# Retention and MLP on one core: the scores of two chunks issued back to back, the second pair of PSUM banks taken from the MLP ring

## The chip, the cores and the metric

The kernel runs on one core of a Trainium2 chip. A core has TensorE (PE: matmuls into PSUM; weight loads are listed as PEld), VectorE (DVE), ScalarE (ACT), GpSimd (POOL) and SyncE (SP, which here only issues DMAs). PSUM has eight banks of 128 x 512 fp32 values. Each engine takes its instructions in order, and engines wait for one another on semaphores. The metric is the device time of one execution in microseconds (us).

## The reference, cut to what matters

There are 4 batches of 768 positions. The first half is a retention layer with 8 heads of 64 dimensions; the second a low-rank mix along the sequence and an MLP of 512 to 2048 to 512 with a residual.

```
state = gamma[h] * state + outer(k[:, :, t], v[:, :, t])      # for each t
y[:, :, t] = q[:, :, t] @ state / sqrt(64)
x = y with the heads side by side                             # (4, 768, 512)
u = x + (x.T @ U @ V).T
out = u + relu(u @ w_ch1) @ w_ch2
```

The kernel computes the retention in six chunks of 128 positions: with q and k scaled by powers of gamma, a chunk's output is its causally masked scores (k times q) applied to v, plus q applied to the state that the chunks before have summed up.

## The kernel before, in words

Batch 0 has its own start, in blocks of 256 positions. After it the program runs four rounds, b = 1 to 4 (the last `for` of the function). A round computes the MLP of batch b - 1 as a list of pieces (`mlp_pieces`), and the steps of the retention and the low-rank part of batch b are put between the pieces. `weave` does this by position: each piece has a cost in us as written in the code, each step a mark given as a share of the round, and a step is issued ahead of the first piece that begins at or after its mark. So the order of the instructions is fixed in the program, and nothing is rearranged at run time.

Five kinds of step belong to a chunk `(b, ci)`. `prep_chunk` scales and casts q, k and v on GpSimd (L267, L269) from tiles of the ring `in`, which the SP queue fills. `turn_dma` (L433) makes `qkT` from `qkd` by a transposing DMA; in batch 2 it is issued by ScalarE's queue, in batch 3 by SP's. `state` (L445) adds the chunk to the state in PSUM and copies it out on ScalarE (L85). `score` (L461) makes eight matmuls of 64 rows by 128, one for each head, even heads into one PSUM bank and odd heads into another; two operations on VectorE then multiply each bank by the causal mask and write `a0` and `a1` (L466). `mix` makes four matmuls of q with the state (L476) and eight of `a` with v (L481) in one bank, and ScalarE copies that to `x` (L85). All other matmuls in these stages use the full 128 rows, except those of the low-rank part (L499, L512).

The MLP's pieces: an up piece is four matmuls into one bank (L678), 512 positions wide or 256 wide, and a relu that writes `gT`: every fourth relu is on VectorE (L683), the others on ScalarE (L685); in round 1 it is every third. From batch 1 on the down product is made with seven block products in place of eight (L600), for which VectorE makes sums and differences of `gT` blocks (`g_sums`, L553, tiles `gS` and `gT`). These sums are chained to certain up pieces.

PSUM is dealt out by hand: `bank(tag)` rotates through a list of banks. In rounds 2 to 4 the ring `mlp` has the banks 6, 0, 1 and 2, `s` has 3 and 4, `o` has 5 and `st` has 7; the down products A, B and C use 6 and 0, 1, and 2. A matmul that starts a new use of a bank waits for the last reader of the use before.

The marks of round b are in `at` (one for each chunk) and `lag` (for the steps `state`, `score` and `mix` of a chunk). The change touches the score, the relu's choice of engine and the marks:

```
at = [0.04 + 0.085 * i for i in range(NCK)]
lag = [0.12, 0.17, 0.23] if b == 2 else [0.1, 0.12, 0.2]
```

Of the kernel before, what the change touches and what calls it, by code (L numbers as in the profile page):

```python
# [18 lines left out]
def kernel(  # L19
# [52 lines left out]
    def bank(tag, dtype=fp32):  # L72
        n_bank[0] += 1
        ring = RINGS[tag]
        ring.append(ring.pop(0))
        return psum.tile([P, 2048 // (4 if dtype == fp32 else 2)], dtype,
                         tag=f"bank{ring[-1]}", name=f"{tag}_{n_bank[0]}",
                         bufs=1)

    def four(t):  # L80
        return t.rearrange("p (n m) -> p n m", n=4)
# [147 lines left out]
    for i in range(NST):  # L229
        t = consts.tile([P, 4, P], bf16, name=f"state{i}")  # L230
# [3 lines left out]
    def causal(t):  # L234
        return t[:, None, :].to_broadcast([P, 4, P])
# [217 lines left out]
                evac("A", ns[r, :, r], four(st_p)[r, :, r])  # L453
            live["state", b] = ns

    def score(b, ci):
        vb, qkT, state = live[b, ci]
        sp = [bank("s") for _ in range(2)]
        for h in range(H):
            r = ds(D * (h % 2), D)  # L460
            nc.tensor.matmul(sp[h % 2][:, ts(h // 2, P)], qkT[r, 4 + h // 2],  # L461
                             qkT[r, h // 2], start=True, stop=True)
        for i in range(2):
            a = rmid.tile([P, 4, P], bf16, tag=f"a{i}", bufs=2,
                          name=f"a{i}_{b}_{ci}")
            nc.vector.tensor_tensor(a, four(sp[i]), causal(mask), op=ALU.mult)  # L466
            live[b, ci].append(a)

    def mix(b, ci):
        if ci == 0:  # L470
# [81 lines left out]
    def part(f, *args):  # L552
        return lambda: f(*args)  # L553
# [8 lines left out]
    def chain(*fs):  # L562
        def f():
            for g in fs:
                g()
        return f
# [100 lines left out]
    def mlp_pieces(b):  # L667
        gT = gtp.tile([P, NM, S], fp16, tag="gT", name=f"gT_{b}")
        pieces = []
        n = [0]  # L670

        def up(m, lo, sz):
            j, nj = lo // P, sz // P

            def f():
                g_p = bank("mlp")
                for c in range(NCB):
                    nc.tensor.matmul(g_p[:, :sz], w1b[:, c, ts(m, P)],  # L678
                                     uTs[b][:, ds(j, nj), c],
                                     start=(c == 0), stop=(c == NCB - 1))  # L680
                n[0] += 1
                if n[0] % (3, 4, 4, 4)[b] == 0:
                    nc.vector.tensor_relu(gT[:, m, ds(lo, sz)], g_p[:, :sz])  # L683
                else:
                    nc.scalar.activation(gT[:, m, ds(lo, sz)], g_p[:, :sz],  # L685
                                         AF.Relu)
            return f

        lo = [(0.864, up(m, 0, LO)) for m in range(NM)]
        hi = [(0.432, up(m, LO, S - LO)) for m in range(NM)]  # L690
        if b < SEVEN:
            pieces += lo + hi
        else:
            gS = gtp.tile([P, 3, NH, TH], fp16, tag="gS", name=f"gS_{b}")

            def quad(t, i):
                return [t[i], t[i + 1], t[i + NH], t[i + NH + 1]]

            def late(steps, at, fs):
                for i, f in enumerate(fs):  # L700
                    cost, g = steps[at + i]
                    steps[at + i] = (cost, chain(g, f))

            for t, i in ((lo, 0), (lo, 2), (hi, 0), (hi, 2), (lo, 4), (hi, 4),
                         (lo, 6), (hi, 6)):
                pieces += quad(t, i)
            late(pieces, 12, g_sums(gT, gS, 0))
            late(pieces, 16, g_sums(gT, gS, 2))
            late(pieces, 24, g_sums(gT, gS, 4))
            s1, s2, s3, s4 = g_sums(gT, gS, 6)  # L710
            late(pieces, len(pieces) - 1, [chain(s1, s2)])
            down = down_pairs(b, gT, gS)
            late(down, 0, [s3, s4])
            return pieces + down
        hold = {}

        def down(j, m0):
            def f():
                if m0 == 0:
                    hold[j] = bank("mlp")  # L720
                ch = hold[j]
                for m in range(m0, m0 + 4):
                    nc.tensor.matmul(ch, gT[:, m, ts(j, P)], w2b[:, m],  # L723
                                     start=(m == 0), stop=(m == NM - 1))
                if m0 == NM - 4:
                    o_sb = outp.tile([P, DM], fp32, tag="o_sb",
                                     name=f"o_{b}_{j}")
                    nc.vector.tensor_tensor(o_sb, ch, us[b][:, j], op=ALU.add)
                    dst = out[b, ts(j, P)]
                    if b:  # L730
                        stores.append((nc.scalar, dst, o_sb))
                    else:
                        for i in range(2):
                            stores.append((nc.sync, dst.rearrange(
                                "(p two) c -> two p c", two=2)[i],
                                o_sb[ds(HP * i, HP)]))
            return f

        for j in range(NCK):
            for m0 in range(0, NM, 4):  # L740
                pieces.append((0.864, down(j, m0)))
        return pieces
# [108 lines left out]
    for b in range(1, B + 1):  # L851
        tracks = []
        if b > 1:
            old = b - 1 < SEVEN
            first = [part(lr_expand, b - 1, 4, 2, "qk" if old else "st"),
                     part(lr_turn_pe, b - 1, 4, "qk" if old else "o")
                     if b < 3 else part(lr_turn, b - 1, 4)]
            if not old:
                RINGS["mlp"] = [6, 0, 1, 2]
        tracks.append((first, 0.02, (0.2, 0.14, 0.1, 0.06)[b - 1]))  # L860
        if b < B:
            if b == 1:
                at = [0.475, 0.575, 0.63, 0.69, 0.745, 0.8]
                lag = [0.01, 0.035, 0.065]
                turn = turn_pe
                for i in range(AHEAD, NCK):
                    tracks.append(([part(prep_chunk, b, i)], at[i] - 0.1, 1))
                tracks.append(([order_v], at[-1] - 0.05, 1))
                for f, d in zip(w2_sums(0) + w2_sums(2),
                                (0.515, 0.53, 0.55, 0.6, 0.655, 0.67, 0.715,  # L870
                                 0.73)):
                    tracks.append(([f], d, d))
            else:
                for i in range(NCK):
                    prep_chunk(b, i)
                at = [0.04 + 0.085 * i for i in range(NCK)]
                lag = [0.12, 0.17, 0.23] if b == 2 else [0.1, 0.12, 0.2]
                if b == 2:
                    for i, f in enumerate(w2_sums(4) + w2_sums(6)):
                        d = 0.04 + 0.025 * i  # L880
                        tracks.append(([f], d, d))
                turn = turn_dma
            for i in range(NCK):
                for f, d in ((turn, 0), (state, lag[0]), (score, lag[1]),
                             (mix, lag[2])):
                    tracks.append(([part(f, b, i)], at[i] + d, at[i] + d))
            t = at[-1] + lag[2]
            if b == 1:
                tracks += [([part(lr_open, b), part(lr_proj, b)], t + 0.02,
                            t + 0.02),  # L890
                           ([part(lr_expand, b, 0, 4)], t + 0.04, t + 0.04),
                           ([part(lr_turn_pair, b, 0, "A"),
                             part(lr_turn_pair, b, 2, "D")], t + 0.08, t + 0.12)]
            else:
                for fs, d in (([part(lr_open, b), part(lr_proj, b)], 0.03),
                              ([part(lr_grow, b, 0, 4, "st")], 0.06),
                              ([part(lr_add, b, 0, 4, (0, 1))], 0.06),
                              ([part(lr_add, b, 0, 4, (2, 3))], 0.11),
                              ([part(lr_turn, b, 0)], 0.17),
                              ([part(lr_turn, b, 2)], 0.171)):  # L900
                    tracks.append((fs, t + d, t + d))
        weave(mlp_pieces(b - 1), *tracks)
# [29 lines left out]
```

## Time and profile before

Four executions were timed; the profiled one took the same time as the lowest of them.

| what | value |
|---|---|
| median of 4 runs | 224.35 us |
| lowest and highest | 223.83 and 226.71 us |
| the profiled execution | 223.83 us |
| its span from first to last instruction | 221.2 us |
| round 2's up pieces (MLP of batch 1, chunks of batch 2) | about 82 to 109 us, chunks up to 118 us |
| round 3's up pieces (MLP of batch 2, chunks of batch 3) | about 131 to 157 us, chunks up to 165 us |
| eight score matmuls, L461, each | 216 ns, two at a time |
| mask, L466, 128 x 512 | 680 ns (median) |
| relu of 512 columns: ScalarE L685, VectorE L683 | 597 ns, 686 ns (mean, 82 to 170 us) |
| sums of 128 x 768, L553 | about 550 ns |

In the lines of a timeline the first number is the start in us from the start of the span, the second the length; then engine, line, operation, what is written and read, the shape, and how many instructions are merged. In brackets stands how long the engine was idle before, and what ended that. Matmuls overlap, and their ends are modelled, so starts tell more than lengths. ACTq and SPq are the queues of ScalarE and SP that issue DMAs. In a group of the page, "128*128" is the size of the array that a matmul uses and the next figures its operand.

### The profile page before, as it was taken

Reading aid. Unit: us, or ns where it says so; the run is one execution under the profiler, and the core shown is the slowest. Engines: PE = TensorE matmul, PEld = TensorE weight load, DVE = VectorE, ACT = ScalarE, POOL = GpSimd, SP = SyncE. Lnnn points to the kernel's source line nnn. Section 1 sums busy time; section 2 is a strip of 40 time slices with the busy share of each in tenths; the row PEclk is TensorE's granted clock in tenths of the full one; section 3 lists DMA queues with packets and bytes.
Section 4 is the critical chain, followed back from the end, with each engine's and each line's share of the span. In section 5 each row is a group of like instructions: output and inputs, shape, how many; then the busy total and the mean of one; then the engine's idle time right before and its main releaser. Section 6 shows DMA issues by size and latency. Waiting matters only on the chain. (4 is left out here: it accounts for less than half of the span.)

```text
span 221.2 us, 5593 instructions
## 1 busy us (share of the span) xinstructions
PE 214.0 (97%) x2275; PEld 151.3 (68%) x2275; DVE 142.7 (65%) x293; ACT 88.4 (40%) x182; POOL 85.4 (39%) x123
## 2 busy tenths in 40 slices
PE   7989999999999999999999999999999999999993
PEld 7868854485656554666788874766888846668882
DVE  7488665335766378699795843886868452857542
ACT  3247545465464315567611015666320035550000
POOL 6458888778779665325658202000000000000000
PEclk9999999999999999999999999999999999999999
DMA  6999999999999999999999499720002731000123
GB/s 168 302 279 282 286 373 261 365 334 204 214 220 222 197 233 213 277 189 197 240 206 213 161 229 234 143 50 0 3 0 98 190 123 22 0 1 3 47 105 133
DMA packets 93369, 38.82 MB, mean 176 GB/s; under 512 B 76864, under 2 KB 86176, under 8 KB 93344
## 3 DMA queue, kind: packets, MB, share of 16 engines
q1 hardware_dynamic: 86144, 35.33, 67.9%
q10 hardware_dynamic: 7200, 3.15, 7.1%
q8 instruction: 17, 0.28, 0.6%
q14 instruction: 8, 0.07, 0.1%
HBM read 27.46 MB, written 6.29 MB: 153 GB/s over the span
## 5 line engine op out<-in xcount | busy, mean ns | idle before, releaser
L678 PE MATMUL mlp<-uT,w1b 128*128 128x512 f16 (+1 forms) x512 | 89.6, 326 | 0.2 <-DMA uT<-x 0.2
L685 ACT ACTIVATE gT<-mlp 128x512 f16<-128x512 f32 (+1 forms) x94 | 45.6, 491 | 63.1 <-PE mlp L678 59.3
L678 PEld LDWEIGHTS <-w1b 128*128 128x128 f16 x512 | 48.0, 98 | 30.7 <-DMA uT<-x 0.7
L683 DVE TENSOR_SCALAR gT<-mlp 128x512 f16<-128x512 f32 (+1 forms) x34 | 18.9, 555 | 27.4 <-PE mlp L678 27.4
L600 PEld LDWEIGHTS <-gT 128*128 128x128 f16 x288 | 27.6, 98 | 3.6
L466 DVE TENSOR_TENSOR a<-s,mask 128x512 bf16<-128x512 f32 x36 | 23.1, 683 | 8.8 <-PE s L461 8.8
L269 POOL TENSOR_TENSOR qkd<-in,gk 128x512 bf16<-128x512 f32 x18 | 19.2, 1066 | 18.1 <-DMA in<-in_k_dram 17.6
L723 PE MATMUL mlp<-w2b,gT 128*128 128x512 f16 x96 | 24.1, 380 | 0.0
L269 POOL TENSOR_TENSOR qkd<-in,gq 128x512 bf16<-128x512 f32 x18 | 19.4, 1080 | 11.9 <-DMA in<-in_q_dram 10.1
L600 PEld LDWEIGHTS <-gS 128*128 128x128 f16 x216 | 20.9, 98 | 3.0 <-issue 0.5
L85 ACT ACTIVATE x<-o 128x512 f16<-128x512 f32 x20 | 11.9, 594 | 19.4 <-PE o L481 18.9
L600 PE MATMUL A<-w2t,gT 128*128 128x256 f16 x144 | 18.4, 273 | 0.0
L85 ACT ACTIVATE state<-st 64x256 bf16<-64x256 f32 x40 | 15.0, 375 | 4.5 <-PE st L358 3.1
L267 POOL CAST vd<-in 128x512 bf16<-128x512 f32 x18 | 11.3, 627 | 6.2 <-DMA in<-in_v_dram 3.7
L723 PEld LDWEIGHTS <-gT 128*128 128x128 f16 x96 | 8.2, 98 | 7.5
L173 PE MATMUL mlp<-ones 128*128 128x128 bf16 x136 | 11.4, 252 | 1.4 <-DVE ones L166 1.4
L173 PEld LDWEIGHTS <-ones 128*128 128x128 bf16 x152 | 11.0, 114 | 2.2 <-DVE ones L166 1.4
L321 POOL CAST w2b<-in 128x512 f16<-128x512 f32 x16 | 9.8, 616 | 2.9 <-DMA in<-in_moe_w_ch_dram 2.2
L518 DVE TENSOR_TENSOR x<-s,x 128x256 f16<-128x256 f32 (+1 forms) x16 | 8.2, 551 | 3.1 <-PE st L512 1.9
L315 POOL CAST w1b<-in 128x512 f16<-128x512 f32 x16 | 9.6, 617 | 1.4 <-DMA in<-in_moe_w_ch_dram 1.1
L85 ACT ACTIVATE qkT<-qk 128x1024 bf16<-128x1024 bf16 x6 | 6.1, 1024 | 8.7 <-PE qk L425 8.7
L600 PE MATMUL C<-w2t,gS 128*128 128x256 f16 x72 | 9.3, 273 | 0.0
(136 smaller groups left out, 271.5 us busy)
## 6 DMA issues: line engine op xcount, KB each, us to landing
in<-in_moe_w_ch_dram SPq DMA_DIRECT2D x32, 256.0 KB, 6.0
in<-in_k_dram SPq DMA_DIRECT2D x24, 256.0 KB, 5.3
in<-in_q_dram SPq DMA_DIRECT2D x24, 256.0 KB, 5.4
in<-in_v_dram SPq DMA_DIRECT2D x24, 256.0 KB, 5.6
out_dram<-o SPq DMA_DIRECT2D x12, 256.0 KB, 2.0
out_dram<-o SPq DMA_DIRECT2D x12, 128.0 KB, 3.4
out_dram<-o ACTq DMA_DIRECT2D x6, 256.0 KB, 3.0
Uf<-in_moe_U_dram SPq DMA_DIRECT2D x1, 96.0 KB, 5.1
```

The source lines that it names most:

```text
L85: nc.scalar.activation(dst, src, AF.Copy)
L173: nc.tensor.matmul(idle_bank[0][:, ts(i % 4, P)], ones[:, :P], ones[:, :P], start=True, stop=True, skip_group_check=True)
L267: nc.gpsimd.tensor_copy(out=t, in_=src)
L269: nc.gpsimd.tensor_tensor(t, src, g[:, ci, :, None].to_broadcast([P, H, D]), op=ALU.mult)
L315: nc.gpsimd.tensor_copy(out=w1b[:, c, ts(mb, 512)], in_=take("w1", mb, c))
L321: nc.gpsimd.tensor_copy(out=w2b[:, m], in_=take("w2", m))
L466: nc.vector.tensor_tensor(a, four(sp[i]), causal(mask), op=ALU.mult)
L600: nc.tensor.matmul(acc[key, i], lhs[:, m, ts(i, P)], rhs[:, m], start=(fresh and m == 0), stop=(m == NH - 1), skip_group_check=True)
L678: nc.tensor.matmul(g_p[:, :sz], w1b[:, c, ts(m, P)], uTs[b][:, ds(j, nj), c], start=(c == 0), stop=(c == NCB - 1))
L683: nc.vector.tensor_relu(gT[:, m, ds(lo, sz)], g_p[:, :sz])
L685: nc.scalar.activation(gT[:, m, ds(lo, sz)], g_p[:, :sz], AF.Relu)
L723: nc.tensor.matmul(ch, gT[:, m, ts(j, P)], w2b[:, m], start=(m == 0), stop=(m == NM - 1))
```

## The change

`score` is split: the matmuls, which now take a tag for their banks, and `screen`, the two masks, which is returned as a function to call later. For batch 1 and for chunks 4 and 5, `score_one` does both at once, as before. For chunks 0 to 3 of batches 2 and 3, `score_two` issues the matmuls of chunk `ci` into the banks `s` and those of chunk `ci + 1` into two banks of the ring `mlp`, and then the four masks. It stands where the score of the odd chunk stood. The mixes of both chunks come after it, at marks 0.05 and 0.09 later. For the three up pieces that follow a pair, a counter keeps the relu on ScalarE where it would have been VectorE's turn; the turn is then VectorE's at a later piece.

```
-    def score(b, ci):
+    def score(b, ci, tag="s"):
         vb, qkT, state = live[b, ci]
-        sp = [bank("s") for _ in range(2)]
+        sp = [bank(tag) for _ in range(2)]
         for h in range(H):
             r = ds(D * (h % 2), D)
             nc.tensor.matmul(sp[h % 2][:, ts(h // 2, P)], qkT[r, 4 + h // 2],
                              qkT[r, h // 2], start=True, stop=True)
+        return part(screen, b, ci, sp)
+
+    def screen(b, ci, sp):
         for i in range(2):
             a = rmid.tile([P, 4, P], bf16, tag=f"a{i}", bufs=2,
                           name=f"a{i}_{b}_{ci}")
             nc.vector.tensor_tensor(a, four(sp[i]), causal(mask), op=ALU.mult)
             live[b, ci].append(a)
+
+    spare = [0]
+
+    def score_one(b, ci):
+        score(b, ci)()
+
+    def score_two(b, ci):
+        for f in [score(b, ci), score(b, ci + 1, "mlp")]:
+            f()
+        spare[0] = 3
...
                 n[0] += 1
+                if spare[0]:
+                    spare[0] -= 1
+                    n[0] -= n[0] % (3, 4, 4, 4)[b] == 0
                 if n[0] % (3, 4, 4, 4)[b] == 0:
                     nc.vector.tensor_relu(gT[:, m, ds(lo, sz)], g_p[:, :sz])
                 else:
...
             for i in range(NCK):
-                for f, d in ((turn, 0), (state, lag[0]), (score, lag[1]),
-                             (mix, lag[2])):
-                    tracks.append(([part(f, b, i)], at[i] + d, at[i] + d))
+                steps = [(turn, at[i]), (state, at[i] + lag[0])]
+                if b == 1 or i > 3:
+                    steps += [(score_one, at[i] + lag[1]), (mix, at[i] + lag[2])]
+                else:
+                    t = at[i | 1] + lag[1]
+                    if i % 2:
+                        steps.append((mix, t + 0.09))
+                    else:
+                        steps += [(mix, t + 0.05)]
+                        tracks.append(([part(score_two, b, i)], t + 1e-6,
+                                       t + 1e-6))
+                for f, d in steps:
+                    tracks.append(([part(f, b, i)], d, d))
```

## The prediction

> **What bounds the kernel now.** I read the page's busy shares first, then the timeline of TensorE through one stage, then of the other engines in the same stretch.
>
> ```profile
> PE 214.0 (97%) x2275; PEld 151.3 (68%) x2275; DVE 142.7 (65%) x293; ACT 88.4 (40%) x182; POOL 85.4 (39%) x123
> ```
>
> TensorE is busy for 97% of the span, so whatever makes it wait or work less shows in the time at once; the others have slack on average. Its timeline tells what a score block costs (start, length, line, form, count):
>
> ```profile
> 92.98 0.40 PE L461 MATMUL s<-qkT 64*128 64x128 bf16 x8
> 93.31 1.48 PE L678 MATMUL mlp<-uT,w1b 128*128 128x256 f16 x12
> 94.63 0.39 PE L445 MATMUL st<-vd,qkd 128*128 128x128 bf16 x4
> ...
> 96.39 1.03 PE L678 MATMUL mlp<-uT,w1b 128*128 128x512 f16 x4
> 97.35 0.40 PE L461 MATMUL s<-qkT 64*128 64x128 bf16 x8
> 97.68 1.04 PE L678 MATMUL mlp<-uT,w1b 128*128 128x512 f16 x4
> 98.55 0.39 PE L445 MATMUL st<-vd,qkd 128*128 128x128 bf16 x4
> ```
>
> Starts are the thing to read. A group of four 512-wide matmuls takes 98.55 - 97.68 = 0.87 us, but the one ahead of the score takes 97.35 - 96.39 = 0.96: entering the score costs 0.10. The score takes 0.33 until the next full-array matmul; its eight matmuls run two at a time on the two row halves, four steps of 0.055, so leaving costs another 0.10. A 256-wide group takes 1.32/3 = 0.44, the state update 0.22.
>
> VectorE in the same stretch, with GpSimd:
>
> ```profile
> 96.81 0.55 DVE L553 TENSOR_TENSOR gS<-gT,gS 128x768 f16<-128x768 f16 x1
> ...
> 97.07 1.19 POOL L269 TENSOR_TENSOR qkd<-in,gk 128x512 bf16<-128x512 f32 x1 [5.98 <-DMA in<-in_k_dram]
> 97.28 1.40 DVE L553 TENSOR_TENSOR gS<-gT 128x768 f16<-128x768 f16 x1
> ...
> 98.71 0.56 DVE L553 TENSOR_TENSOR gS<-gS,gT 128x768 f16<-128x768 f16 x1
> ...
> 99.19 1.28 DVE L466 TENSOR_TENSOR a<-s,mask 128x512 bf16<-128x512 f32 x2
> ```
>
> The sum that began at 97.28 took 1.40 in place of 0.55: it ended 0.41 after the GpSimd multiply (97.07 + 1.19 = 98.26). So the masks of the score at 97.35 began 1.8 us late, which cost nothing, because only the score's own two banks were held.
>
> **What the Trainium skill says.** *TensorEngine Tiling (Array Packing)*, Key Properties: changing the tiling mode drains TensorE. The trace agrees, with 0.10 on the way in and 0.10 out. *PSUM — Partial Sum Buffer*, PSUM bank collisions: guard PSUM by bank, so a matmul into a bank waits for that bank's last reader; here a 256-wide group began at 92.02, just after the relu of its bank (91.37 + 0.60). *TensorE: Matmul & The Clock Gate*, queue depths: matmuls stay in order, and ScalarE and VectorE are strict FIFO; so one held group holds all behind it. *SBUF — State Buffer*, Who interferes with whom: a VectorE operation with two SBUF inputs contends with a GpSimd one that reads SBUF, and the later blocks. The 1.40 above is that.
>
> **The change part by part.**
>
> *Switches removed.* Four pairs (two in batch 2, two in batch 3), each saving one way in and one out: 4 x (0.096 + 0.093) = 0.76 us of TensorE, all on the path. The sixteen matmuls of a pair take 0.33 + 4 x 0.055 = 0.55 from its first to the next full-array matmul.
>
> *Two ring banks held.* In batches 2 and 3 the ring of the up products has four banks. The second score of a pair takes two. They come free with the third and fourth mask, since VectorE takes the four in order. The first mask starts 0.45 after the score (93.43 against 92.98); two masks take 1.28 at 0.68 each, so starts are 0.60 apart. If VectorE is free, the third ends 0.45 + 2 x 0.60 + 0.68 = 2.33 after the pair began and, with 0.04 for the release (91.97 to 92.01, above), its bank can be written at 2.37. When does TensorE want it? The order of instructions after each pair gives the work in between:
> - Batch 2, chunks 0 and 1: a 512 group, the state update, a 512 group, the mix of chunk 0 (0.24), then the group that needs the bank: 0.55 + 0.87 + 0.22 + 0.87 + 0.24 = 2.75. In time, by 0.38.
> - Batch 2, chunks 2 and 3: two 256 groups and the state update: 0.55 + 0.88 + 0.22 = 1.65. Short by 0.72.
> - Batch 3, chunks 0 and 1: a 256 and a 512 group: 1.86. Short by 0.51.
> - Batch 3, chunks 2 and 3: two 512 groups: 2.29. Short by 0.08.
>
> The sum is 1.31, with VectorE free. The fourth mask (2.97) is met each time, since another group or a mix lies before its bank is wanted.
>
> *VectorE not free.* At the second pair of batch 2 the masks stand behind a sum, a 512-wide relu and three more sums. Adding up the queue: ScalarE issues the transpose of chunk 4 and copies a mix ahead of the relu that the first sum needs, so that sum starts near 103.3; then 0.60 (relu ready at 103.9), 0.60, and 3 x 0.47 bring the masks to 105.97, when the scores (begun 105.5) are just ready. But GpSimd works through batch 3's inputs then, at times that its DMAs set:
>
> ```profile
> 102.89 1.04 POOL L269 TENSOR_TENSOR qkd<-in,gk 128x512 bf16<-128x512 f32 x1
> 104.71 0.69 POOL L267 CAST vd<-in 128x512 bf16<-128x512 f32 x1 [0.78 <-DMA in<-in_v_dram]
> 105.91 1.04 POOL L269 TENSOR_TENSOR qkd<-in,gq 128x512 bf16<-128x512 f32 x1 [0.51 <-DMA in<-in_q_dram]
> ```
>
> Each sum that starts inside one of them ends 0.41 after it. The first sum then ends at 104.34, the second at 105.81, the fourth at 107.36, and the masks begin at 107.28, 1.31 late. Bounds: 0 if none collide, 1.9 (the delay seen at 97.28 to 99.19) at worst; I take 1.31. In batch 3 GpSimd ends at 134.4, ahead of the first sum there (141.3), and the same addition leaves the masks no more than 0.05 late.
>
> *Relus moved.* Up to three groups after a pair go to ScalarE, three relus in all (0.60 each). ScalarE is busy 18.8 of 37 us in that stage; cost 0. They matter in one place: the relu order behind the transpose, in the second rival.
>
> *Scores and mixes moved.* Chunk 0's score used to stand ahead of a group (93.31) that waits for ScalarE's relu; without that 0.43 of cover the group waits 0.16. The mix of chunk 1, which waited 0.11 at 100.5 for its mask, now comes with the mask long done: -0.11. Other moved mixes find masks and state ready; 0, bounded by 0.2 either way. The transposes keep their place among GpSimd's and SP's work; only ScalarE's DMA queue is reordered.
>
> Sum: -0.76 + 1.31 + 1.31 + 0.16 - 0.11 = +1.91 us. The profiled execution took 223.83 (span 221.2 and 2.6 around it), which gives 225.7. The median of the runs shown is 0.5 above it: 226.2.
>
> **The rivals.**
> *No collision with GpSimd.* The input DMAs land at other times, or GpSimd is the one to wait. The second pair of batch 2 costs 0.72 alone: +0.6, so 224.95. Against it: three GpSimd operations of 1.04, 0.69 and 1.04 lie in 4 us.
>
> *The transpose holds ScalarE longer.* It issues them in its own order:
>
> ```profile
> 97.45 0.60 ACT L685 ACTIVATE gT<-mlp 128x512 f16<-128x512 f32 x1
> ...
> 97.53 2.42 ACTq L433 DMA_TRANSPOSE qkT<-qkd  x1
> ...
> 100.00 0.60 ACT L685 ACTIVATE gT<-mlp 128x512 f16<-128x512 f32 x1 [1.95 <-PE mlp L678]
> ```
>
> Of the six on this queue five take about 1.3 and this one 2.42; no relu starts meanwhile. Now it would issue at 97.0, right at the first pair, with a relu, the state copies, a relu and the copy of mix 0 behind it. At 1.3 that copy is done by 100.7, in time. At 2.42 it ends at 99.47 + 0.50 + 0.76 + 0.50 + 0.60 = 101.83, and the mix of chunk 1, which needs that single bank at 100.86, waits 1.0. Half is given back at the second pair, where TensorE comes later: +2.4, so 226.75, slower by over 1%.
>
> *Not slower: the masks free the banks in time.* Then only the switches count: -0.76, so 223.6. The place is the group after the two up groups in three of the four pairs. It decides at a third mask that ends before 1.65 to 1.86 after the pair's start, against 2.33 from the rows. The first mask cannot start before 0.45 and three at 0.60 follow, so it needs masks of half their length; or the wait would have to fall where TensorE waits already, and none is there.
>
> **How the numbers follow.** Forecast (+1.4 to +2.2) 0.55; no collision 0.19; longer hold 0.20; banks in time 0.06. About 1% (2.2 us) is what a measurement of this kernel tells from no change; the forecast lies inside it and above zero. Over 1% slower needs 226.6: most of the longer hold and the forecast's upper edge, 0.29. Over 1% faster: 0.01. The range goes from 224.6 (no collision, less 0.3 of scatter) to 227.3 (longer hold, plus 0.5).
>
> **What would show it.** Right: score blocks of sixteen matmuls, 0.55 to the next full-array matmul; a gap of 1.5 to 2 us on TensorE before an up group after the second pair of batch 2, about 0.5 after the first of batch 3, all released by the masks; none after the first of batch 2. Wrong: such gaps missing, or gaps behind ScalarE. What would make it wrong most: GpSimd's operations at other times.

## The result and the profile after

The changed kernel took 226.7 us (median of 38 runs), the kernel before 224.68 (59 runs) beside it: a ratio of 1.0051, 95% interval 1.0031 to 1.0072, which is +1.15 us (0.70 to 1.62). The medians are over all executions, and lie 2.0 us apart; the ratio, here and in the experiments, leaves out the executions that are more than 1.5% above the fastest of their kernel. A second measurement (the first experiment) gave 1.0092 (1.0059 to 1.0125), +2.07 us. The forecast was +1.9 us and 226.2. So the change makes the kernel slower by 0.5 to 0.9%. That is inside the 1% that the prediction took for the least that a measurement can tell from no change, but both intervals leave out 1.

The profiled execution took 229.62 us (span 227.8, mean TensorE clock 0.983): TensorE waited 3.57 us up to 94.8 us, ahead of every instruction that the change moves, and the granted clock was about half from 94 us to 100.7 (last section). Its total is therefore not set against the 223.83 us of before; its stretches around the pairs, at full clock, are. The busy shares of the page:

```profile
PE 215.3 (95%) x2275; PEld 151.8 (67%) x2275; DVE 140.6 (62%) x290; ACT 89.6 (39%) x185; POOL 84.1 (37%) x123
```

The counts show the moved relus: in all three fewer operations on VectorE, three more on ScalarE. TensorE's share fell from 97 to 95%, but most of that is the wait at 94.8.

The timeline of the changed kernel around the first pair of batch 2 (start, length, engine, line, form, count):

```profile
102.31 0.40 PE L461 MATMUL s<-qkT 64*128 64x128 bf16 x8
...
102.86 1.04 PE L691 MATMUL mlp<-uT,w1b 128*128 128x512 f16 x4
...
103.95 1.28 DVE L469 TENSOR_TENSOR a<-mlp,mask 128x512 bf16<-128x512 f32 x2
...
105.06 1.48 PE L691 MATMUL mlp<-uT,w1b 128*128 128x256 f16 x12
```

Sixteen score matmuls take 102.86 - 102.31 = 0.55 us to the next full-array matmul. The third mask (103.95) is done at 104.63, and the group that takes its bank begins at 105.06 without a wait.

The second pair of batch 2:

```profile
110.54 0.66 POOL L267 CAST vd<-in 128x512 bf16<-128x512 f32 x1 [0.23 <-DMA in<-in_v_dram]
110.65 0.96 DVE L566 TENSOR_TENSOR gT<-gT 128x768 f16<-128x768 f16 x1
111.03 0.40 PE L461 MATMUL s<-qkT 64*128 64x128 bf16 x8
...
112.00 1.28 DVE L469 TENSOR_TENSOR a<-s,mask 128x512 bf16<-128x512 f32 x2
112.47 0.39 PE L445 MATMUL st<-vd,qkd 128*128 128x128 bf16 x4
...
113.20 1.27 DVE L469 TENSOR_TENSOR a<-mlp,mask 128x512 bf16<-128x512 f32 x2
...
113.92 0.60 PE L691 MATMUL mlp<-uT,w1b 128*128 128x256 f16 x4 [1.07 <-DVE a L469]
```

The last line names the releaser: VectorE's mask `a`. The state update began at 112.47 and takes 0.22, so the group was wanted at 112.69 and began at 113.92: TensorE lost 1.23 us. (The 1.07 in brackets counts from a modelled end of the matmuls; starts are exact.) The masks began at 112.00, where an idle VectorE would have begun at 111.03 + 0.45 = 111.48: 0.52 late, behind two sums, one of which took 0.96 beside the GpSimd cast at 110.54.

The first pair of batch 3:

```profile
148.12 0.40 PE L461 MATMUL s<-qkT 64*128 64x128 bf16 x8
148.28 0.55 DVE L566 TENSOR_TENSOR gT<-gT 128x768 f16<-128x768 f16 x1
...
148.75 1.28 DVE L469 TENSOR_TENSOR a<-s,mask 128x512 bf16<-128x512 f32 x2
149.95 1.28 DVE L469 TENSOR_TENSOR a<-mlp,mask 128x512 bf16<-128x512 f32 x2
150.69 0.59 PE L691 MATMUL mlp<-uT,w1b 128*128 128x512 f16 x2 [0.54 <-DVE a L469]
```

Wanted at 148.12 + 1.86 = 149.98, begun at 150.69: 0.71 lost. A sum (148.28) stood ahead of the masks, which began 0.63 after the scores in place of 0.45. After the second pair of batch 3 the group with the third mask's bank waits 0.08: from the first matmul of the three groups of 512 after the pair to the one behind them it is 2.68 us (157.67 to 160.35), and 2.60 where no group waits.

### The profile page after: what moved, and what is told of

It reads as the page before. It is cut to its first block, busy times and chain, and to the rows that moved or that the text cites. A ratio compares the mean times of both kernels' runs of the same rounds, so it can differ in the third digit from the quotient of the medians.

```text
span 227.8 us, 5589 instructions
## 1 busy us (share of the span) xinstructions
PE 215.3 (95%) x2275; PEld 151.8 (67%) x2275; DVE 140.6 (62%) x290; ACT 89.6 (39%) x185; POOL 84.1 (37%) x123
## 5 line engine op out<-in xcount | busy, mean ns | idle before, releaser
L691 PE MATMUL mlp<-uT,w1b 128*128 128x512 f16 (+1 forms) x512 | 92.0, 333 | 5.3 <-ACT gT L701 3.6
L691 PEld LDWEIGHTS <-w1b 128*128 128x128 f16 x512 | 49.5, 100 | 37.1 <-issue 6.2
L701 ACT ACTIVATE gT<-mlp 128x256 f16<-128x256 f32 (+1 forms) x97 | 46.9, 492 | 68.8 <-PE mlp L691 61.3
L699 DVE TENSOR_SCALAR gT<-mlp 128x256 f16<-128x256 f32 (+1 forms) x31 | 17.1, 553 | 35.5 <-PE mlp L691 35.4
L469 DVE TENSOR_TENSOR a<-s,mask 128x512 bf16<-128x512 f32 x28 | 18.0, 683 | 7.0 <-PE s L461 7.0
L173 PE MATMUL mlp<-ones 128*128 128x128 bf16 x136 | 10.7, 243 | 1.4 <-DVE ones L166 1.4
L173 PEld LDWEIGHTS <-ones 128*128 128x128 bf16 x152 | 10.3, 110 | 2.2 <-DVE ones L166 1.4
L613 PE MATMUL B<-w2b,gT 128*128 128x256 f16 x72 | 9.3, 273 | 0.0
```

The costliest lines, as they stand in the source:

```text
L173: nc.tensor.matmul(idle_bank[0][:, ts(i % 4, P)], ones[:, :P], ones[:, :P], start=True, stop=True, skip_group_check=True)
L613: nc.tensor.matmul(acc[key, i], lhs[:, m, ts(i, P)], rhs[:, m], start=(fresh and m == 0), stop=(m == NH - 1), skip_group_check=True)
L691: nc.tensor.matmul(g_p[:, :sz], w1b[:, c, ts(m, P)], uTs[b][:, ds(j, nj), c], start=(c == 0), stop=(c == NCB - 1))
L701: nc.scalar.activation(gT[:, m, ds(lo, sz)], g_p[:, :sz], AF.Relu)
```

## The experiments

Two theories were put to the test. **Masks:** what is lost is TensorE's wait for the ring banks whose masks VectorE takes third and fourth, longer where VectorE comes late. **ScalarE:** the loss is behind ScalarE, its transposes and the relus and copies queued after them. A "pair" is one block of sixteen score matmuls. In each run, "lost" is the start of a group of matmuls, less the start of the matmul ahead of it and that one's own step; masks are "late" by what their start lies beyond 0.45 us after the first score matmul. Differences in us are the ratio's distance from 1 times the median of before in that series.

### The changed kernel once more

No edit.

> The changed kernel once more, on the chip of the next three runs. Mask theory (the up group after a pair waits for the third mask): gaps on TensorE of 1.0 to 2.0 us after the second pair of batch 2, 0.5 after the first of batch 3, below 0.15 after the other two; each pair saves 0.19; ratio to before 1.003 to 1.007. ScalarE theory (relus and mixes moved behind the transposes on ScalarE's queue cost the time): gaps that end with a relu of ScalarE or a copy of a mix, after the first pair of batch 2 too, and the mask gaps short.

Measured: 1.0092 (1.0059 to 1.0125), +2.07 us (1.33 to 2.81). This execution ran without the long wait near 94 us. Its timeline, first at batch 2's first pair (a GpSimd multiply, a sum, the masks and the group that waits), then at the second:

```profile
97.94 1.23 POOL L269 TENSOR_TENSOR qkd<-in,gk 128x512 bf16<-128x512 f32 x1 [6.43 <-DMA in<-in_k_dram]
...
98.19 1.40 DVE L566 TENSOR_TENSOR gS<-gT 128x768 f16<-128x768 f16 x1
...
100.10 1.28 DVE L469 TENSOR_TENSOR a<-s,mask 128x512 bf16<-128x512 f32 x2
...
102.03 1.19 PE L691 MATMUL mlp<-uT,w1b 128*128 128x256 f16 x8 [0.30 <-DVE a L469]
...
107.77 1.30 POOL L269 TENSOR_TENSOR qkd<-in,gq 128x512 bf16<-128x512 f32 x1 [0.56 <-DMA in<-in_q_dram]
...
108.08 1.40 DVE L566 TENSOR_TENSOR gS<-gT,gS 128x768 f16<-128x768 f16 x1
108.16 0.40 PE L461 MATMUL s<-qkT 64*128 64x128 bf16 x8
...
109.40 1.27 DVE L469 TENSOR_TENSOR a<-s,mask 128x512 bf16<-128x512 f32 x2
...
111.33 0.60 PE L691 MATMUL mlp<-uT,w1b 128*128 128x256 f16 x4 [1.34 <-DVE a L469]
```

At both pairs a sum of 1.40 ended 0.41 after a GpSimd multiply (107.77 + 1.30 + 0.41 = 109.48 = 108.08 + 1.40). At the first pair (scores at 98.78, masks at 100.10) the masks began 1.32 after the scores, 0.87 late; 0.38 of that was spare, and the group lost 0.47, the next one, which needs the fourth mask's bank, 0.16. At the second pair they were 0.79 late and the group lost 1.51. The first pair of batch 3 lost 0.71 again. So the waits of batch 3 repeat to the hundredth, and those of batch 2 follow where GpSimd's operations fall, at the first pair too. Two expectations missed: the first pair was to lose less than 0.15, and the ratio lies above the 1.003 to 1.007.

### The banks swapped

The first score of each pair takes the ring's banks, so their masks come first and second:

```
-        for f in [score(b, ci), score(b, ci + 1, "mlp")]:
+        for f in [score(b, ci, "mlp"), score(b, ci + 1)]:
```

> The first score of each pair goes to the two MLP banks and the second to the banks s, nothing else moves. Mask theory: the MLP banks are free after the first and second mask, at 1.17 and 1.77 us after the pair's start where they are wanted at 1.65 to 1.86 and later, so the gaps of 0.5 and 0.1 in batch 3 go and that of batch 2's second pair shrinks to what VectorE is behind, less 0.5: 0 to 0.8. The switches stay saved (0.76). Ratio to before 0.996 to 1.001. ScalarE theory: its queue is as in the changed kernel, so the ratio stays at 1.003 to 1.007.

Measured: 0.9994 (0.9967 to 1.0022), -0.13 us (-0.74 to +0.49). The timeline at batch 3's first pair, then at batch 2's second:

```profile
145.32 0.40 PE L461 MATMUL mlp<-qkT 64*128 64x128 bf16 x8
...
145.87 2.34 PE L691 MATMUL mlp<-uT,w1b 128*128 128x256 f16 x12
145.95 1.28 DVE L469 TENSOR_TENSOR a<-mlp,mask 128x512 bf16<-128x512 f32 x2
```

```profile
107.68 0.40 PE L461 MATMUL mlp<-qkT 64*128 64x128 bf16 x8
...
108.02 1.39 DVE L566 TENSOR_TENSOR gS<-gT,gS 128x768 f16<-128x768 f16 x1
...
109.34 1.27 DVE L469 TENSOR_TENSOR a<-mlp,mask 128x512 bf16<-128x512 f32 x2
...
110.06 0.60 PE L691 MATMUL mlp<-uT,w1b 128*128 128x256 f16 x4 [0.56 <-DVE a L469]
```

In batch 3 the twelve matmuls after the pair run on without a gap, though the masks begin just as late (0.63): the order of the banks alone takes the 0.71 away. ScalarE's work is the same as in the changed kernel, and its theory wanted 1.003 to 1.007 where the interval ends at 1.0022, so the theory of ScalarE falls. At batch 2's second pair 0.72 is still lost: VectorE came 1.21 late (scores at 107.68), behind a sum of 1.39 beside a GpSimd multiply. With the old order of banks that lateness would have cost 0.72 + 1.21 = 1.93 (an estimate from the 0.72 of a free VectorE). So the swap helps at this place too, but does not make it free.

### Pairs in batch 3 alone, and in batch 2 alone

```
-                if b == 1 or i > 3:
+                if b < 3 or i > 3:
```

> Pairs in batch 3 alone, batch 2 as before. Mask theory: two pairs save 0.38 us, the gaps are 0.51 and 0.08, so +0.2 us, ratio 1.001. ScalarE theory: no transposes are on ScalarE's queue in batch 3, so nothing is lost: -0.4 us, 0.998.

Measured: 1.0036 (1.0005 to 1.0067), +0.81 us (0.11 to 1.51). The group after the first pair in the timeline:

```profile
147.16 1.02 PE L691 MATMUL mlp<-uT,w1b 128*128 128x512 f16 x4 [0.54 <-DVE a L469]
```

With the pair at 144.59 it loses 147.16 - 144.59 - 1.86 = 0.71, as with all four pairs. The expectation had 0.51 here and missed by the same 0.2. Two pairs save 0.38, and 0.71 + 0.08 goes: +0.41, inside the interval. The 0.998 of ScalarE's theory is outside it.

```
-                if b == 1 or i > 3:
+                if b != 2 or i > 3:
```

> Pairs in batch 2 alone, batch 3 as before. Mask theory: two pairs save 0.38 us, the second has a gap of 1.0 to 2.0, the lost cover of 0.16 and the wait of 0.11 that goes: +0.7 to +1.7 us, ratio 1.003 to 1.008. ScalarE theory: the whole loss of the changed kernel is here, with the gaps after ScalarE's relus or copies.

Measured: 1.0050 (1.0018 to 1.0082), +1.12 us (0.40 to 1.84). In this execution the masks of the second pair began 1.26 late, and the group lost 1.98:

```profile
109.25 1.34 POOL L269 TENSOR_TENSOR qkd<-in,gk 128x512 bf16<-128x512 f32 x1
109.62 1.39 DVE L566 TENSOR_TENSOR gT<-gT 128x768 f16<-128x768 f16 x1
...
109.69 0.40 PE L461 MATMUL s<-qkT 64*128 64x128 bf16 x8
...
111.40 1.27 DVE L469 TENSOR_TENSOR a<-s,mask 128x512 bf16<-128x512 f32 x2
...
113.33 0.60 PE L691 MATMUL mlp<-uT,w1b 128*128 128x256 f16 x4 [1.82 <-DVE a L469]
```

The gap ends with a mask, not with a relu or a copy of ScalarE. The two halves together, 0.81 + 1.12 = 1.93, lie between the two measurements of the whole, 1.15 and 2.07: each batch has its own share of the loss.

### GpSimd's operations made short

In batch 3 GpSimd works on one head of eight, with the tiles of batch 2, so seven eighths of batch 3's scaling are left out; the order of all other engines stays. Parts of the edit:

```
+        w = slice(0, 1) if b == 3 else slice(0, H)
...
-                nc.gpsimd.tensor_copy(out=t, in_=src)
+                nc.gpsimd.tensor_copy(out=t[:, w], in_=src[:, w])
...
-                    t, src, g[:, ci, :, None].to_broadcast([P, H, D]),
+                    t[:, w], src[:, w],
+                    g[:, ci, w, None].to_broadcast([P, w.stop, D]),
```

> The changed kernel, but in batch 3 GpSimd scales and casts only one head of the eight of each chunk (the tiles of batch 2 are used again), so GpSimd's operations in batch 2's second pair shrink from 0.7 to 1.2 us to some 0.1 to 0.2; seven eighths of batch 3's scaling are left out. TensorE, VectorE and ScalarE get the same instructions in the same order. If VectorE comes late at that pair because sums are blocked by GpSimd, the first mask of the pair now begins 0.45 to 0.55 after the scores, the group after the two 256-wide ones waits 0.7 to 0.85 us (with the collisions it was 1.2, 1.5 and 2.0 in three executions), and the time is 0.5 to 1.2 us below the changed kernel, 225.7 to 226.4 or about the time before. If VectorE is late because of its own queue (sums behind relus), the wait stays between 1.2 and 2.0 and the time stays at 226.9. The wait after batch 3's first pair stays at 0.7 in both, since GpSimd has ended there.

Measured: 1.0009 (0.9970 to 1.0048), +0.20 us (-0.68 to +1.08). The lines are numbered seven higher in this kernel. The timeline at batch 2's second pair:

```profile
107.06 0.40 PE L468 MATMUL s<-qkT 64*128 64x128 bf16 x8
...
107.39 0.33 POOL L275 TENSOR_TENSOR qkd<-in,gq 128x64 bf16<-128x64 f32 x1 [0.70 <-DMA in<-in_q_dram]
107.50 1.29 DVE L476 TENSOR_TENSOR a<-s,mask 128x512 bf16<-128x512 f32 x2
...
109.44 0.60 PE L698 MATMUL mlp<-uT,w1b 128*128 128x256 f16 x4 [0.55 <-DVE a L476]
```

The sums ahead of the masks take 0.54 to 0.59, the masks begin 0.44 after the scores, and the group loses 0.71, which is the 0.72 worked out for a free VectorE. This is one execution, but the others say the same: what the sums ahead of the masks took beyond 0.55 each adds up to 0.56 us in the changed kernel, 0.85 in its second profile and 1.31 with pairs in batch 2 alone, where the masks were 0.52, 0.79 and 1.26 late. So GpSimd's operations are what made VectorE late in these. The loss is in every execution about 0.72 plus what the masks are late:

| kernel, batch 2's second pair | masks late | group lost |
|---|---|---|
| changed, with short GpSimd operations | 0.00 | 0.71 |
| changed | 0.52 | 1.23 |
| changed, no relu moved (below) | 0.73 | 1.45 |
| changed, again | 0.79 | 1.51 |
| pairs in batch 2 alone | 1.26 | 1.98 |

GpSimd's work is shorter in the preparation of all of batch 3, so the time of this kernel is not a price of that one wait.

### No relu moved

```
-        spare[0] = 3
+        spare[0] = 0
```

> The changed kernel, but no relu is moved to ScalarE: every fourth stays VectorE's. If the move costs and gains nothing, as was predicted, the time is the changed kernel's within 0.3 us (226.6 to 227.2) and the waits after the pairs are the same. Rival: a relu in VectorE's queue near a pair lies ahead of masks or sums, so the wait after batch 2's second pair grows by a relu, 0.6 to 0.7, or a ring bank comes back 0.3 to 1 us later behind four masks; then the time is 0.5 us or more above.

Measured: 1.0069 (1.0038 to 1.0099), +1.55 us, between the two measurements of the changed kernel. So moving the relus is worth nothing that these runs can see. The waits are of the same size (1.45 at batch 2's second pair, 0.71 in batch 3), but at the former they have another cause, as the timeline shows:

```profile
109.02 0.40 PE L461 MATMUL s<-qkT 64*128 64x128 bf16 x8
109.13 0.69 DVE L699 TENSOR_SCALAR gT<-mlp 128x512 f16<-128x512 f32 x1 [1.39 <-PE mlp L691]
...
110.20 1.28 DVE L469 TENSOR_TENSOR a<-s,mask 128x512 bf16<-128x512 f32 x2
...
112.13 0.60 PE L691 MATMUL mlp<-uT,w1b 128*128 128x256 f16 x4 [1.28 <-DVE a L469]
```

VectorE had been idle for 1.39 us until the group ahead of the pair was done; its relu and a sum of 0.55 after it then put the masks 0.73 late, with none of these sums stretched by GpSimd. The rival's relu on top of the collisions did not come: in this execution the one delay took the place of the other.

### Three pairs, and two, with the ring's banks first

The order of banks of the swapped kernel; no pair at batch 2's chunks 2 and 3, where the swapped kernel still lost 0.72 us, more than a pair saves:

```
-                if b == 1 or i > 3:
+                if b == 1 or i > 3 or (b == 2 and i > 1):
```

> Pairs at batch 2's chunks 0 and 1 and at both places of batch 3, none at batch 2's chunks 2 and 3, and the first score of each pair takes the banks of the MLP ring (whose masks come first). Theory of the masks: the ring's banks are free about 1.75 after the pair began at the latest, against 1.86 or later wanted, so no group waits for a mask; three pairs save 3 x 0.19 = 0.57 us, the cover lost in batch 2 takes 0.16 to 0.2 back, the mix of chunk 1 no longer waits 0.11: 0.4 to 0.5 us below before, a ratio of 0.998. Rival, the saved switches are eaten by other waits however the banks are dealt: no change or slower, a ratio of 1.000 to 1.003, with waits of 0.2 or more in round 2 or 3 that before does not have.

> The same kernel as the one with three pairs and the ring's banks first, measured once more because its first ratio, 0.9968, has an interval that ends at 0.9993. Theory of the masks: three pairs save 0.57 us, less 0.1 to 0.2 of lost cover: a ratio of 0.997 to 0.998, and no wait for a mask after a pair. Rival: the first measurement was luck of the order, and the ratio is 1.000 or above.

Measured: 0.9968 (0.9943 to 0.9993) and, again, 0.9960 (0.9927 to 0.9993): -0.7 and -0.9 us, medians of 224.30 and 224.20. The timeline at batch 2's first pair in the second of these executions:

```profile
98.22 0.40 PE L461 MATMUL mlp<-qkT 64*128 64x128 bf16 x8
...
99.22 1.27 DVE L469 TENSOR_TENSOR a<-mlp,mask 128x512 bf16<-128x512 f32 x2
...
100.96 0.71 PE L691 MATMUL mlp<-uT,w1b 128*128 128x256 f16 x5
```

The masks begin 1.00 after the scores, 0.55 late, which would have cost 0.17 with the old order of banks; the group at 100.96 does not wait, nor does any after the pairs of batch 3. This version is faster than the kernel before by 0.3 to 0.4%: little, but both intervals leave out 1.

Two pairs, in batch 3 alone, with the ring's banks first:

```
-        for f in [score(b, ci), score(b, ci + 1, "mlp")]:
+        for f in [score(b, ci, "mlp"), score(b, ci + 1)]:
...
-                if b == 1 or i > 3:
+                if b < 3 or i > 3:
```

> Pairs in batch 3 alone, the first score of each in the banks of the MLP ring. Theory of the masks: no wait for a mask (with the banks s first it was 0.7), so the two pairs save 2 x 0.19 = 0.38 us, a ratio of 0.998, and about 1.4 us less than was measured with pairs in batch 3 alone and the banks s first. Rival, the saved time is lost elsewhere: ratio 1.000 or above, with a wait of 0.2 or more after a pair of batch 3.

Measured: 0.9976 (0.9947 to 1.0005), -0.54 us (-1.19 to +0.11): the ratio is near the 0.998 expected, but not told apart from no change. No group after batch 3's pairs loses 0.2 us; against pairs in batch 3 with the old order of banks (+0.81) it is 1.35 us less, where the traces account for 0.79; the two were measured in different series, and their intervals leave room for the rest.

## Why the prediction was right

The direction, the mechanism and the total held; some terms were mis-sized, in opposite senses, so that the total is closer than its parts. By its steps:

- **Switches removed, -0.76.** Right: 0.55 us from a pair's first matmul to the next full-array one, at every pair; 0.096 on the way in (97.35 - 96.39, less the group's 0.87), once in place of twice. The sum itself is a little low: by the prediction's own lengths two blocks take 2 x (0.096 + 0.33) and a pair 0.096 + 0.55, so a pair saves 0.206, and four save 0.82. The 0.38 and 0.57 of the experiments carry the same difference.
- **Third mask's bank, VectorE free.** First pair of batch 2 in time: right in the first execution (104.63 against 105.06, by 0.39 with the release at 0.04; forecast 0.38). Second pair 0.72: 0.71 with GpSimd out of the way. Second pair of batch 3, 0.08: measured 0.08. First pair of batch 3, 0.51: measured 0.71 in each of the five executions that have this pair with the old order.
- **Batch 3, "the same addition leaves the masks no more than 0.05 late".** This failed: they were 0.18 late at the first pair, since the sum that begins just ahead of them (148.28) has 0.47 to run before the next operation starts. It is 0.2 of the 0.71.
- **VectorE not free, 1.31.** The mechanism was right (sums that end 0.41 after a GpSimd operation, masks behind them), the size too large in two of three executions: 0.52, 0.79 and 1.26. The prediction laid the GpSimd rows of before over the new order as if they stayed in place; the DMAs land elsewhere in each execution, within the bounds of 0 to 1.9 that it gave. It took the first pair as free of this. In three of the five executions with the old order of banks it was not: the group with the third mask's bank lost 0.47 (the second profile), 0.30 (no relu moved: scores at 99.74, group at 102.79) and 0.18 (short GpSimd operations, where this pair still meets a full multiply of batch 2: 98.00 and 100.93), and the next group waited 0.16 each time for the fourth mask, which was to be met each time.
- **Relus moved, 0.** Right in the time. That without the move a relu stands ahead of the masks at the second pair was not foreseen.
- **Lost cover, 0.16.** Eight executions have batch 2's first pair. The second group after the wait near 94 us lost 0.20 in five of them; in three it lost nothing (in two TensorE had not waited there first, in the changed kernel's own the clock was at half). The mix of chunk 1 did not wait, as said.

For the first execution the terms make -0.76 + 1.23 + 0.71 + 0.08 - 0.11 = +1.15, against +1.15 measured; for the second -0.76 + 0.47 + 0.16 + 1.51 + 0.71 + 0.08 - 0.11 = +2.06 (the 0.16 is the wait for the fourth mask after the first pair), against +2.07. With 0.82 for the switches they make +1.09 and +2.00. One execution stands for many there, and the first itself took 229.62 us for a reason outside this sum, so the closeness is partly luck. That batch 2's waits differ from execution to execution is shown; how much of the spread of the times comes from them is not, since the wait near 94 us differs by more (last section).

**The rivals.** *No collision*, +0.6, did not come about by itself; the kernel with short GpSimd operations shows its wait of 0.71. *The transpose holds ScalarE longer*: at the first pair ScalarE's transpose took 1.25 us in both executions, and the longest from there on in any kernel with that pair was 1.30; the 2.42 of before did not come back, and no group after a pair waited for ScalarE. *Banks in time*: refuted for the change as it is; in batch 3 it is what the swapped order brings about.

*PSUM — Partial Sum Buffer* of the Trainium skill, section PSUM bank collisions, on which the step rested, asks that a program guard PSUM by bank. The traces show that guard at work: the group began 0.04 to 0.06 us after the end of the mask that read its bank (113.20 + 0.68 = 113.88, then 113.92) at each pair where it waited.

**What stays open.** How often GpSimd falls in with the sums at each pair was seen in a few executions only. No kernel was tried in which the sums of batch 2 are moved away from the second pair, which might make the fourth pair pay as well.

## What to carry to other kernels

When a producer borrows buffers from a ring that another engine needs soon, give it the buffers that will be freed first: here swapping which score takes the ring's banks turned 0.71 us of waiting at batch 3's first pair to none, with the same instructions. Compare, at each place, when the last reader frees the buffer with the work that lies before its next use; here a margin of 0.38 us was not safe, since VectorE's queue came up to 0.87 late at that pair. Saving 0.2 us of switches per pair is worth it only where that comparison comes out well with the queue in its worst observed state.

## What was not expected of the hardware

A wait near 92 to 95 us, ahead of anything that the change touches, differs from execution to execution: counted by starts it is 0.2 us in the kernel before, none, 0.4, 1.4, 1.5 and 2.6 to 3.0 in others, among them two kernels whose round 2 is that of before (2.6 and 2.9). ScalarE's relu there stands behind a transpose that waits, as the profile reads it, for GpSimd's product. In the changed kernel's profile it was the longest, 3.7; the relu began at 94.12 after 4.93 us of waiting, and in the timeline the group follows:

```profile
94.77 1.44 PE L691 MATMUL mlp<-uT,w1b 128*128 128x256 f16 x6 [3.57 <-ACT gT L701]
```

The busy time of each engine in the six microseconds after it (PE with its sum first, PEld, DVE, ACT, POOL; then the granted clock, DMA share and GB/s):

```profile
94.80:101.00 6.20, 6.20 (x31) 4.22 (x31) 2.74 (x7) 3.41 (x10) 1.33 (x2) 0.52 1.13 220
```

The clock was at 0.52 over that stretch and 1.00 over the seven microseconds after it, and 256-wide matmuls started 0.213 us apart in place of 0.109. *TensorE: Matmul & The Clock Gate*, section What's actually happening, puts the drop to half after about 3.4 us of idleness. The longest wait had a drop, but the others do not follow that figure:

| kernel | wait by starts | granted clock |
|---|---|---|
| pairs in batch 3 alone, ring's banks first | 2.6 | 0.50 from 94 to 97 us |
| pairs in batch 3 alone, banks s first | 2.9 | 1.00 from 94.7 to 98 us |
| pairs in batch 2 alone | 2.9 | 0.50 from 96 to 98 us |
| no relu moved | 3.0 | 1.00 from 95 to 98 us |
| changed | 3.7 | 0.50 from 94 to 100 us |

In the first of these rows the clock fell while TensorE was still waiting (0.96 from 93 to 94 us, with the matmuls back at 94.19), in the third only after it had begun again at 94.48 (0.75 from 95 to 96). So two waits below 3.4 us came with half the clock and two of like length did not: in these runs the length of one wait does not tell whether the clock falls. What decides it stays open.
